# o and dq with V and K as the moving operand in a one-core attention backward kernel

## The chip, the cores and the metric

The kernel runs on one core of a Trainium2 chip. A core has TensorE (PE in the profile, PEld for its weight loads), VectorE (DVE), ScalarE (ACT), GpSimd (POOL) and SyncE (SP); the last two mostly order transfers here. The metric is the device time of one execution in microseconds, lower is better.

## What is computed

A decode step and its gradients: one token, attention over a cache of 4096 keys in 32 heads of 128, a dense layer with the mish activation beside it, and a gate that mixes both. The forward part:

```python
def _A_ref(x, k_cache, v_cache, wq, wo):
    B, Sq, D = x.shape
    H, Dh = 32, 128
    q = (lambda x, *d: x.transpose(*d))((x @ wq).reshape(B, Sq, H, Dh), 0, 2, 1, 3)
    scores = jnp.einsum("bhqd,bhkd->bhqk", q, k_cache) * (Dh ** -0.5)
    p = _softmax(scores, axis=-1)
    o = jnp.einsum("bhqk,bhkd->bhqd", p, v_cache)
    return (lambda x, *d: x.transpose(*d))(o, 0, 2, 1, 3).reshape(B, Sq, H * Dh) @ wo
...
x = A_x
g = _sigmoid((x * gate_w).sum(-1, keepdims=True))
a = _A_ref(x, A_k_cache, A_v_cache, A_wq, A_wo)
b = _B_ref(x, B_w1, B_b1, B_w2)
return g * a + (1 - g) * b
```

The outputs are this value and, by `jax.vjp` with a given `grad_out`, the gradients of x, both caches and all weights. Per head that means, with do the gradient of o: dP = V do, ds = p (dP - sum of dP p), dK = ds q, dV = p do, and dq = K^T ds. D is 640, everything is in bfloat16. K, V, dK and dV are 1 MB per head each and make up most of the traffic.

## The kernel before

One period of the loop (`period(h)`) treats one head. Its K and V lie in SBUF as 128 partitions x 32 columns of keys (J = 32) x 128 (Dh): key p*32 + j is at partition p, column j. Each of kts and vts has four buffers; the loads of head h+3 are ordered on SP's queue before period h, and a load waits until the last reader of its buffer is done. For K that reader is the dq product, for V the o product.

The order on each engine is written out by hand (`manual_schedule`); every engine works through its own list in order. The steps of one period:

- Scores of the next head. K is transposed on TensorE in four chunks of four FP32 transposes, each of which carries a pair of bfloat16 columns (`transposes`, lines 575 to 583). ACT copies a chunk out of PSUM as tT (line 582), and eight products (`products`, line 589) with 48 moving columns write the scores to the PSUM tile sA. `k_chunk` and `s_chunk` do this for head h+1 during period h. The same is done with V of head h, as `V(c)` and `dP(c)`, into the tile sB.
- Softmax of head h: the maximum m (line 664), its transpose over partitions (668), negM (670), e = exp(S - M) (675), the sum Z by a product with ones (678), zs (680), 1/Z as rz (682), p (684).
- o (`o_part`, line 660): 32 products accumulate in one PSUM region. Column j of V (128 x 128) is the stationary operand, column j of e is the moving one, broadcast to W = 48 equal columns, of which one is used. In the same way dq (line 713) takes K and ds.
- pj (691) sums dP times e, PT (694) transposes the partial sums, dj (700) adds them, ds (702) follows.
- dV and dK are outer products on VectorE, in two halves each (line 605); dK of head h is made in period h+1. Their stores go out on POOL's queue.
- `slot(h)` takes a few steps out of a list of other work (the dense layer, q, the gradients of wq and wo) on TensorE and VectorE.

sA has two buffers and sB one; each is one PSUM bank of 512 FP32 columns, in which scores, Z, o and the transpose of m, or dP, dq and PT, have their own columns.

Of the kernel before, what the change touches and what calls it, by code (L numbers as in the profile page):

```python
# [8 lines left out]
ALU = mybir.AluOpType  # L9
AX = mybir.AxisListType  # L10
F32 = mybir.dt.float32
# [5 lines left out]
def kernel(  # L17
# [24 lines left out]
    nc = tc.nc  # L42
    P = 128
    _, H, Sk, Dh = A_k_cache.shape
    D = A_x.shape[-1]
    F = B_w1.shape[1]
    J = Sk // P
    RC = D // P
    G = 4
    W = 48  # L50
# [40 lines left out]
    small = ctx.enter_context(tc.tile_pool(name="small", bufs=3))  # L91
# [21 lines left out]
    kts, vts, wqs, wos = {}, {}, {}, {}  # L113
# [26 lines left out]
    def load_w2(c):  # L140
# [25 lines left out]
    ident_f = const.tile([P, P], F32, name="ident_f")  # L166
    nc.gpsimd.memset(ident_f[:], 0.0)
    nc.gpsimd.affine_select(
        out=ident_f[:], in_=ident_f[:], compare_op=ALU.not_equal, fill=1.0,
# [69 lines left out]
    for i in range(3):  # L239
        t = const.tile([P, 2, G, 2, 2], BF16, name=f"qd2_{i}")  # L240
# [13 lines left out]
    def slot(h, p=2, d=1):  # L254

        slot_no[0] += 1
        room = {"P": p, "D": d, "T": 99}
        for kind in ("T", "D", "P"):
            for st in list(steps):
                name, k, fn, deps, head = st  # L260
                if k != kind or head > h or not room[k]:
                    continue
                if all(done.get(x, 1 << 30) < slot_no[0] for x in deps):
                    fn()
                    done[name] = slot_no[0]
                    steps.remove(st)
                    room[k] -= 1
# [63 lines left out]
    o_all = const.tile([P, H], BF16, name="o_all")  # L331
    dq_all = const.tile([P, H], BF16, name="dq_all")
# [242 lines left out]
    def transposes(src, c):  # L575
        tp = tr_ps.tile([P, 4, P], F32, name="tr", tag="tr")
        flat = f32v(src[:].rearrange("p j d -> p (j d)"))
        for t in range(4):
            k = c * 4 + t
            nc.tensor.transpose(tp[:, t, :], flat[:, k * P:(k + 1) * P], ident_f[:])  # L580
        sb = tsb.tile([P, 4, P], F32, name="tT", tag="tT")
        nc.scalar.copy(sb[:].rearrange("p a b -> p (a b)"), tp[:].rearrange("p a b -> p (a b)"))  # L582
        return sb[:].rearrange("p a b -> p (a b)").bitcast(BF16).rearrange("p (a b two) -> p a two b", a=4, two=2)

    def products(out, tb, c, vec):
        for t in range(4):
            k = c * 4 + t
            for par in range(2):
                nc.tensor.matmul(out[:, 2 * k:2 * k + W], lhsT=tb[:, t, par, :],  # L589
                                 rhs=vec[:, par, :].unsqueeze(1).to_broadcast([P, W // 2, 2]),  # L590
                                 start=(par == 0), stop=(par == 1))

    def k_chunk(h, c, ts):
        ts.append(transposes(kts[h], c))

    def s_chunk(h, c, ts):
        gp = gps[h // G]
        if c == 0:
            sts[h] = {"A": sa_ps.tile([P, 512], F32, name="sA", tag="sA")}
        products(sts[h]["A"][:, 0:J + W], ts[c], c, gp["x2"][:, 0, h % G])  # L600
# [10 lines left out]
    def dk_half(h, half):  # L611
        if h < 0:
            return
        st = sts[h]
        if half == 0:
            st["dK"] = outs.tile([P, J, Dh], BF16, name="dK_sb", tag="dVK")
        outer(st["dK"], st["ds"], gps[h // G]["qd"][:, 0, (h % G) * Dh:(h % G + 1) * Dh], half)
        if h == H - 1:
            a, b = half * (J // 2), (half + 1) * (J // 2)
            ring(h).dma_start(dKv[h][:, a:b, :], st["dK"][:, a:b, :])  # L620
        elif half == 1:
            ring(h).dma_start(dKv[h], st["dK"][:])  # L622
        if half == 1:
            sts.pop(h)

    def dv_half(h, half):
        st = sts[h]
        if half == 0:
            st["dV"] = outs.tile([P, J, Dh], BF16, name="dV_sb", tag="dVK")
        outer(st["dV"], st["p"], gps[h // G]["qd"][:, 1, (h % G) * Dh:(h % G + 1) * Dh], half)  # L630
        if half == 1:
            if h % 7 == 5 and h < H - 3:
                spread(h // 7, dVv[h], st["dV"])
            else:
                ring(h).dma_start(dVv[h], st["dV"][:])  # L635
# [9 lines left out]
    def period(h):  # L645
        gp = gps[h // G]
        st = sts[h]
        nxt = h + 1 < H
        A = st["A"]
        S, Z, O, MM = A[:, 0:J], A[:, 96:96 + J], A[:, 128:128 + W], A[:, 256:384]  # L650
        B = st["B"] = sb_ps.tile([P, 512], F32, name="sB", tag="sB")
        DP, DQ, PT = B[:, 0:J + W], B[:, 128:128 + W], B[:, 256:384]
        vec = gp["x2"][:, 1, h % G]
        tv, tk = [], []
        V = lambda c: tv.append(transposes(vts[h], c))
        dP = lambda c: products(DP, tv[c], c, vec)

        def o_part(a, b):
            for j in range(a, b):
                nc.tensor.matmul(O, lhsT=vts[h][:, j, :], rhs=st["e"][:, j:j + 1].to_broadcast([P, W]),  # L660
                                 start=(j == 0), stop=(j == J - 1))

        m32 = small.tile([P, 1], F32, name="m32", tag="m32")
        nc.vector.reduce_max(m32[:], S, axis=AX.X)  # L664
        V(0)
        dk_half(h - 1, 0)
        V(1)
        nc.tensor.transpose(MM, m32[:].to_broadcast([P, P]), ident_f[:])
        negM = small.tile([P, 1], F32, name="negM", tag="negM")
        nc.vector.tensor_reduce(negM[:], MM, axis=AX.X, op=ALU.max, negate=True)  # L670
        dk_half(h - 1, 1)
        e = st["e"] = small.tile([P, J], BF16, name="e_bf", tag="e_bf")
        V(2)
        dP(0)
        nc.scalar.activation(e[:], S, ACT.Exp, bias=negM[:], scale=1.0)
        V(3)
        dP(1)
        nc.tensor.matmul(Z, lhsT=ones_bf[:], rhs=e[:], start=True, stop=True)
        zs = small.tile([P, 1], F32, name="zs", tag="zs")
        nc.vector.reduce_sum(zs[:], Z, axis=AX.X)  # L680
        rz = st["rz"] = small.tile([P, 1], F32, name="rz", tag="rz")
        nc.vector.reciprocal(rz[:], zs[:])  # L682
        p_bf = st["p"] = small.tile([P, J, 2], BF16, name="p_bf", tag="p_bf")
        nc.scalar.activation(p_bf[:], e[:].unsqueeze(2).to_broadcast([P, J, 2]), ACT.Copy, scale=rz[:])  # L684
        dP(2)
        o_part(0, J)
        dP(3)
        slot(h)
        part = small.tile([P, 1], F32, name="part", tag="part")
        pj = small.tile([P, J], F32, name="pj", tag="pj", bufs=1)  # L690
        nc.vector.scalar_tensor_tensor(pj[:], in0=DP[:, 0:J], scalar=1.0, in1=e[:], op0=ALU.mult, op1=ALU.mult,
                                       accum_out=part[:])
        dv_half(h, 0)
        nc.tensor.transpose(PT, part[:].to_broadcast([P, P]), ident_f[:])  # L694
        if nxt:
            k_chunk(h + 1, 0, tk)
            k_chunk(h + 1, 1, tk)
        dd = small.tile([P, 1], F32, name="dd", tag="dd")
        dj = small.tile([P, P], F32, name="dj", tag="dj", bufs=1)
        nc.vector.tensor_scalar(dj[:], PT, rz[:], None, ALU.mult, ALU.add, accum_out=dd[:])  # L700
        ds = st["ds"] = small.tile([P, J, 2], BF16, name="ds_bf", tag="ds_bf")
        nc.vector.scalar_tensor_tensor(ds[:], in0=DP[:, 0:J].unsqueeze(2).to_broadcast([P, J, 2]), scalar=dd[:], in1=p_bf[:],  # L702
                                       op0=ALU.subtract, op1=ALU.mult)
        dv_half(h, 1)
        nc.vector.tensor_scalar(o_all[:, h:h + 1], O[:, 0:1], rz[:], None, ALU.mult)  # L705
        if nxt:
            s_chunk(h + 1, 0, tk)
            k_chunk(h + 1, 2, tk)
        slot(h)
        if nxt:  # L710
            s_chunk(h + 1, 1, tk)
        for j in range(J):
            nc.tensor.matmul(DQ, lhsT=kts[h][:, j, :], rhs=ds[:, j, 0:1].to_broadcast([P, W]),  # L713
                             start=(j == 0), stop=(j == J - 1))
        if nxt:
            k_chunk(h + 1, 3, tk)
            s_chunk(h + 1, 2, tk)
        nc.scalar.copy(dq_all[:, h:h + 1], DQ[:, 0:1])  # L718
        if nxt:
            s_chunk(h + 1, 3, tk)  # L720
        kts.pop(h)
        vts.pop(h)
        slot(h, 2, 2)
# [131 lines left out]
```

## Time and profile before

| | |
|---|---|
| median of 3 runs | 402.33 us (402.27 to 402.36) |
| the profiled execution | 402.56 us |
| its span, first to last instruction | 400.8 us |
| granted TensorE clock, mean | 0.913 |
| data moved by DMA | 164.92 MB, mean 412 GB/s |
| o products (line 660) | 1024, record of one 183 ns |
| dq products (line 713) | 1024, record of one 183 ns, a few at 215 |
| one head, from m to m | 9.2 to 12.1 us, four heads 15.8 to 21.3 us |

The records of products overlap, as they are pipelined: how fast they run is read from the distance of their starts, not from the length of a record. In the timeline a line has the start and the length in us, the engine, the source line, the operation, what it writes and reads, and in brackets how long the engine stood idle before it and whose end released it. In the waits a line says which instruction waited for which, then the total in us, how often, and the longest. A table of stretches has each engine's busy time in each stretch, the granted clock, the share of the DMA engines and the rate.

### The profile page before, as it was taken

What the parts mean: (1) busy time and instruction counts of PE and PEld (TensorE: products, weight loads), DVE (VectorE), ACT (ScalarE), POOL (GpSimd) and SP (SyncE); (2) the same over time, 40 slices, a digit from 0 to 9 for tenths busy, and PEclk for the clock granted to TensorE, in tenths of its full rate; (3) what the DMA queues carried; (4) which work ended last, traced back from release to release, by engine and by line L of the source; (5) the groups of instructions that cost most, each with busy time, mean ns of one, the idle gap of its engine ahead of it and who ended that gap; (6) DMA issues with size and microseconds to landing.
All of it is one profiled execution on the core that took longest, in us unless ns stands there. A gap on an engine that the chain in (4) does not pass through costs nothing.

```text
span 400.8 us, 13361 instructions
## 1 busy us (share of the span) xinstructions
PE 301.0 (75%) x5752; PEld 266.0 (66%) x5752; DVE 303.1 (76%) x783; ACT 178.2 (44%) x403; POOL 47.0 (12%) x94
## 2 busy tenths in 40 slices
PE   0788888678888788768879788838888888888300
PEld 0577888567777677658868778718777678877200
DVE  3339666556799999767658999836999997898860
ACT  1455454325545555326533555604545545555000
POOL 0001111021110111211110112101111121111000
PEclk9899999959999999969977999967999999999755
DMA  8999999999999999999999999999999999999995
GB/s 292 417 407 405 418 426 421 407 423 421 424 421 424 422 422 416 422 424 424 419 424 426 422 422 417 417 425 424 421 421 424 424 423 418 425 420 418 424 383 229
DMA packets 28359, 164.92 MB, mean 412 GB/s; under 512 B 3260, under 2 KB 3964, under 8 KB 12556
## 3 DMA queue, kind: packets, MB, share of 16 engines
q1 hardware_dynamic: 17136, 93.41, 56.5%
q0 software_dynamic: 11104, 70.64, 42.3%
q8 instruction: 45, 0.74, 0.7%
q14 instruction: 14, 0.11, 0.1%
q10 hardware_dynamic: 60, 0.01, 0.0%
HBM read 82.03 MB, written 82.03 MB: 409 GB/s over the span
## 4 chain that ended last, share of the span: by engine, by line
DVE 38%; DMA 32%; PE 20%; ACT 5%; issue 3%; ACTq 0%; SPq 0%
DMA Kn<-in_A_k_cache_dram 30%; DVE dK_sb L605 9%; DVE dV_sb L605 9%; PE tr L580 8%; DVE junk L378 5%; ACT tT L582 4%; DVE junk L278 3%; PE sA L660 3%; PE sA L589 3%; PE sB L713 3%; DVE junk L530 2%; DVE wo_g L367 1%; DMA vec_rows<-in_gate_w_dram 1%; DVE dj L700 1%; DVE dwq_t L732 1%
## 5 line engine op out<-in xcount | busy, mean ns | idle before, releaser
L582 ACT COPY tT<-tr 128x512 f32<-128x512 f32 x256 | 142.4, 587 | 127.8 <-PE tr L580 126.0
L589 PEld LDWEIGHTS <-tT 128*128 128x128 bf16 x2048 | 79.8, 98 | 40.3 <-ACT tT L582 34.6
L580 PE MATMUL tr<-ident_f,Kn 128*128 128x128 f32 x512 | 81.6, 297 | 9.2 <-DMA Kn<-in_A_k_cache_dram 9.2
L605 DVE TENSOR_TENSOR dV_sb<-p_bf,qd 128x2048 bf16<-128x2048 bf16 x64 | 78.0, 1218 | 0.2 <-issue 0.2
L605 DVE TENSOR_TENSOR dK_sb<-ds_bf,qd 128x2048 bf16<-128x2048 bf16 x64 | 77.7, 1216 | 0.0
L580 PE MATMUL tr<-ident_f,Vn 128*128 128x128 f32 x512 | 72.9, 278 | 0.0
L580 PEld LDWEIGHTS tr<-ident_f,Kn 128*128 128x128 f32 x512 | 61.0, 152 | 10.4 <-issue 10.4
L589 PE MATMUL sA<-qd,tT 128*128 128x48 bf16 x1024 | 48.7, 187 | 23.8 <-ACT dq_all L718 12.7
L580 PEld LDWEIGHTS tr<-ident_f,Vn 128*128 128x128 f32 x512 | 56.3, 142 | 0.0
L589 PE MATMUL sB<-qd,tT 128*128 128x48 bf16 x1024 | 46.0, 183 | 0.0
L660 PEld LDWEIGHTS <-Vn 128*128 128x128 bf16 x1024 | 30.2, 95 | 10.9 <-issue 10.9
L660 PE MATMUL sA<-e_bf,Vn 128*128 128x48 bf16 x1024 | 30.7, 183 | 8.1 <-DVE zs L680 6.5
L622 POOL DMA_DIRECT2D out_dram<-dK_sb x30 | 17.2, 574 | 138.9 <-DVE rz L682 86.5
L713 PE MATMUL sB<-ds_bf,Kn 128*128 128x48 bf16 x1024 | 32.2, 186 | 1.4 <-DVE ds_bf L702 1.4
L664 DVE TENSOR_REDUCE m<-sA 128x1 f32<-128x32 f32 x32 | 6.1, 189 | 32.9 <-PE sA L589 26.4
L713 PEld LDWEIGHTS <-Kn 128*128 128x128 bf16 x1024 | 29.5, 98 | 1.6 <-issue 1.6
L635 POOL DMA_DIRECT2D out_dram<-dV_sb x26 | 14.1, 542 | 135.8 <-DVE o_all L705 53.4
L278 DVE SCALAR_TENSOR_TENSOR junk<-wo_g,da_bc 128x640 bf16<-128x640 bf16 x32 | 26.2, 820 | 1.7 <-ACT da_bc L229 1.1
L378 DVE SCALAR_TENSOR_TENSOR junk<-wq_g,dq_bc 128x1024 bf16<-128x1024 bf16 (+1 forms) x25 | 25.1, 1005 | 0.2
L700 DVE TENSOR_SCALAR_CACHE_REDUCE dj<-sB,rz 128x128 f32<-128x128 f32 x32 | 11.1, 346 | 13.2 <-PE sB L694 13.2
L289 PE MATMUL q_ps<-wq_g,cols_bf 128*128 128x512 bf16 x40 | 13.1, 469 | 10.5 <-DMA wq_g<-in_A_wq_dram 10.5
L684 ACT ACTIVATE p_bf<-e_bf,rz 128x64 bf16<-128x64 bf16 x32 | 11.1, 348 | 13.9 <-DVE rz L682 11.1
(148 smaller groups left out, 268.8 us busy)
## 6 DMA issues: line engine op xcount, KB each, us to landing
Kn<-in_A_k_cache_dram SPq DMA_DIRECT2D x32, 1024.0 KB, 24.0
Vn<-in_A_v_cache_dram SPq DMA_DIRECT2D x32, 1024.0 KB, 28.0
out_dram<-dK_sb POOLq DMA_DIRECT2D x30, 1024.0 KB, 11.8
out_dram<-dV_sb POOLq DMA_DIRECT2D x26, 1024.0 KB, 11.8
wq_g<-in_A_wq_dram SPq DMA_DIRECT2D x4, 1280.0 KB, 23.2
wo_g<-in_A_wo_dram SPq DMA_DIRECT2D x8, 640.0 KB, 17.6
out_dram<-wo_g POOLq DMA_DIRECT2D x7, 640.0 KB, 11.8
out_dram<-dwq_t SPq DMA_DIRECT2D x4, 896.0 KB, 17.5
```

The costliest lines, as they stand in the source:

```text
L278: nc.vector.scalar_tensor_tensor(junk[:, 0:D], in0=wos[g][:, i, :], scalar=1.0, in1=da_bc[:], op0=ALU.mult, op1=ALU.mult, accum_out=gp["do ...
L289: nc.tensor.matmul(q_ps[:], lhsT=x_bf[:, rc:rc + 1].to_broadcast([P, P]), rhs=wq[:, rc, off:off + GD], start=(rc == 0), stop=(rc == RC - 1))
L378: nc.vector.scalar_tensor_tensor(junk[:, c0:c1], in0=wqs[w][:, rc, c0:c1], scalar=1.0, in1=dq_bc[:, w * WG * Dh + c0:w * WG * Dh + c1], op ...
L580: nc.tensor.transpose(tp[:, t, :], flat[:, k * P:(k + 1) * P], ident_f[:])
L582: nc.scalar.copy(sb[:].rearrange("p a b -> p (a b)"), tp[:].rearrange("p a b -> p (a b)"))
L589: nc.tensor.matmul(out[:, 2 * k:2 * k + W], lhsT=tb[:, t, par, :], rhs=vec[:, par, :].unsqueeze(1).to_broadcast([P, W // 2, 2]), start=(pa ...
L605: nc.vector.tensor_tensor(dst[:, a:b, :].rearrange("p j (a b) -> p j a b", b=2), col[:, a:b, :].unsqueeze(2).to_broadcast([P, n, Dh // 2, 2]),
L622: ring(h).dma_start(dKv[h], st["dK"][:])
L635: ring(h).dma_start(dVv[h], st["dV"][:])
L660: nc.tensor.matmul(O, lhsT=vts[h][:, j, :], rhs=st["e"][:, j:j + 1].to_broadcast([P, W]), start=(j == 0), stop=(j == J - 1))
L700: nc.vector.tensor_scalar(dj[:], PT, rz[:], None, ALU.mult, ALU.add, accum_out=dd[:])
L713: nc.tensor.matmul(DQ, lhsT=kts[h][:, j, :], rhs=ds[:, j, 0:1].to_broadcast([P, W]), start=(j == 0), stop=(j == J - 1))
```

## The change

o and dq are now made by `rows2`: two columns of e (or ds) are the stationary operand, two columns of V (or K), 256 elements side by side, are the moving one. Sixteen products accumulate a tile of 2 x 256 in PSUM. Row i, half i of it (the diagonal of 2 x 2 blocks) are the wanted sums over even and odd j; the other two blocks are not used. ACT copies the tile to SBUF as FP32, and `column` turns the two wanted rows into one column of 128 partitions with two FP32 products, whose moving operand is one column of a 2 x 2 identity. The places in the PSUM banks are dealt out anew. For o the column comes after the first `slot(h)`, before the part transpose; for dq it comes between `s_chunk(h + 1, 2)` and `s_chunk(h + 1, 3)`.

```diff
-        S, Z, O, MM = A[:, 0:J], A[:, 96:96 + J], A[:, 128:128 + W], A[:, 256:384]
+        S, Z, O, MM = A[:, 0:J], A[:, 96:96 + J], A[:, 88:89], A[:, 128:256]
+        O2 = A[0:2, 256:512]
         B = st["B"] = sb_ps.tile([P, 512], F32, name="sB", tag="sB")
-        DP, DQ, PT = B[:, 0:J + W], B[:, 128:128 + W], B[:, 256:384]
+        DP, DQ, PT = B[:, 0:J + W], B[:, 88:89], B[:, 128:256]
+        DQ2 = B[0:2, 256:512]
...
-        def o_part(a, b):
-            for j in range(a, b):
-                nc.tensor.matmul(O, lhsT=vts[h][:, j, :], rhs=st["e"][:, j:j + 1].to_broadcast([P, W]),
-                                 start=(j == 0), stop=(j == J - 1))
+        def rows2(out, cols, src):
+            for j in range(0, J, 2):
+                nc.tensor.matmul(out, lhsT=cols[:, j:j + 2], rhs=src[:, j:j + 2, :].rearrange("p j d -> p (j d)"),
+                                 start=(j == 0), stop=(j == J - 2))
+            t = small.tile([2, 2, Dh], F32, name="r2", tag="r2", bufs=2)
+            nc.scalar.copy(t[:].rearrange("i j d -> i (j d)"), out)
+            return t
+
+        def column(out, t):
+            for i in range(2):
+                nc.tensor.matmul(out, lhsT=t[:, i, :], rhs=ident_f[0:2, i:i + 1], start=(i == 0), stop=(i == 1))
...
         dP(2)
-        o_part(0, J)
+        o2 = rows2(O2, e, vts[h])
         dP(3)
         slot(h)
+        column(O, o2)
...
-        nc.vector.tensor_scalar(o_all[:, h:h + 1], O[:, 0:1], rz[:], None, ALU.mult)
+        nc.vector.tensor_scalar(o_all[:, h:h + 1], O, rz[:], None, ALU.mult)
...
-        for j in range(J):
-            nc.tensor.matmul(DQ, lhsT=kts[h][:, j, :], rhs=ds[:, j, 0:1].to_broadcast([P, W]),
-                             start=(j == 0), stop=(j == J - 1))
+        dq2 = rows2(DQ2, ds[:, :, 0], kts[h])
         if nxt:
             k_chunk(h + 1, 3, tk)
             s_chunk(h + 1, 2, tk)
-        nc.scalar.copy(dq_all[:, h:h + 1], DQ[:, 0:1])
+        column(DQ, dq2)
+        nc.scalar.copy(dq_all[:, h:h + 1], DQ)
```

## The prediction, before the changed kernel had run

> **What bounds the kernel now.** I read the page first, then the waits, then nine stretches of the span beside each other, then one undisturbed head in the timeline.
>
> ```profile
> PE 301.0 (75%) x5752; PEld 266.0 (66%) x5752; DVE 303.1 (76%) x783; ACT 178.2 (44%) x403; POOL 47.0 (12%) x94
> PEclk9899999959999999969977999967999999999755
> DMA  8999999999999999999999999999999999999995
> ```
>
> No engine is full, but the DMA row is: 164.92 MB at the 421 to 425 GB/s that most slices show are about 390 us, so transfers leave only some 10 us at the two ends. That looks like a kernel in which nothing else counts. The waits say otherwise:
>
> ```profile
> DVE m L664 <- PE sA L589: 26.4, 13, 5.2
> DVE pj L691 <- PE sB L589: 12.4, 18, 1.1
> PE q_ps L289 <- DMA wq_g<-in_A_wq_dram: 10.5, 3, 5.6
> PE tr L580 <- DMA Kn<-in_A_k_cache_dram: 9.2, 4, 3.3
> ```
>
> After its start the core waits for a load only seven times, 19.7 us in all (columns: total us, times, longest). The rest of the time TensorE (PE) and VectorE (DVE) drive each other, and the DMA is full because its queues hold loads ordered three heads ahead. The two bounds are nearly equal. The stretches show where the difference lies:
>
> ```profile
> core 0: us, PE busy (x) PEld busy (x) DVE busy (x) ACT busy (x) POOL busy (x), PEclk, DMA share, GB/s
> 71.55:90.30 18.75, 13.75 (x207) 11.42 (x206) 11.20 (x32) 5.58 (x12) 3.02 (x5) 0.73 1.02 417
> 162.85:180.00 17.15, 11.11 (x192) 9.63 (x191) 11.50 (x31) 5.58 (x12) 1.85 (x3) 0.80 1.02 423
> 198.60:214.40 15.80, 12.76 (x197) 11.34 (x196) 10.15 (x24) 5.37 (x12) 1.06 (x2) 0.69 1.01 421
> 256.50:277.80 21.30, 12.74 (x189) 10.34 (x187) 11.20 (x32) 5.64 (x12) 1.60 (x3) 0.68 1.02 425
> 277.80:367.30 89.50, 76.16 (x1555) 68.25 (x1553) 83.15 (x196) 47.74 (x108) 13.48 (x22) 1.00 1.01 421
> ```
>
> The first four are heads 5, 13, 16 and 21 (from one m of line 664 to the next). They take 15.8 to 21.3 us; their neighbours take 9.2 to 12.1. Their clock is 0.68 to 0.80, elsewhere it is 1.00: after the wait TensorE runs slowly for a while. What the loads cost is therefore the waits plus the slow work after them. Against similar heads: 18.75 - 10.6 = 8, 5.4 (its two waits, 2.05 + 3.33), 15.8 - 10.9 = 5, 21.3 - 10.9 = 10.5: together 29 us. That is all that a slower computation can hide in. The last row, nine heads (22 to 30), holds none of it: there the computation sets the pace.
>
> One head without a stall, number 15:
>
> ```profile
> 192.25 0.96 PE L660 MATMUL sA<-e_bf,Vn 128*128 128x48 bf16 x32
> 193.05 0.36 PE L589 MATMUL sB<-qd,tT 128*128 128x48 bf16 x8
> 193.45 0.19 DVE L691 SCALAR_TENSOR_TENSOR pj<-sB,e_bf 128x32 f32<-128x32 f32 x1 [1.05 <-PE sB L589]
> 193.70 0.32 PE L694 MATMUL sB<-ident_f,part 128*128 128x128 f32 x1 [0.29 <-DVE pj L691]
> ...
> 196.03 0.96 PE L713 MATMUL sB<-ds_bf,Kn 128*128 128x48 bf16 x32
> 196.83 0.64 PE L580 MATMUL tr<-ident_f,Kn 128*128 128x128 f32 x4
> ...
> 197.56 0.58 ACT L582 COPY tT<-tr 128x512 f32<-128x512 f32 x1 [0.95 <-PE tr L580]
> ...
> 198.20 0.37 PE L589 MATMUL sA<-qd,tT 128*128 128x48 bf16 x8 [0.54 <-ACT dq_all L718]
> ...
> 198.61 0.19 DVE L664 TENSOR_REDUCE m<-sA 128x1 f32<-128x32 f32 x1 [1.97 <-PE sA L589]
> ```
>
> TensorE is dense: o starts at 192.25 and the next group follows 0.80 us later, 32 products at 25 ns; dq the same (196.03 to 196.83). The last products of the next head's scores (198.20) release its m, for which VectorE has waited 1.97 us.
>
> **What the skill says.** "TensorE: Matmul & The Clock Gate", section "Back-to-back issue gap": N moving columns take N/2.4 + 2.5 ns, with a floor of about 25 ns at 64 columns or fewer. The trace agrees on both: 25 ns for these 48 columns, and for 512 columns
>
> ```profile
> 126.08 1.24 PE L289 MATMUL q_ps<-wq_g,cols_bf 128*128 128x512 bf16 x5
> ```
>
> less the 0.377 us record of the last, (1.24 - 0.377)/4 = 216 ns. Section "LDWEIGHTS (loading the stationary operand)": a load is priced by its columns, so two columns cost next to nothing; no load of two columns is in this trace, but those of 128 columns hide beside the products (0.80 us for 32 pairs). Section "Terms" says that transpose mode is four times faster for FP32; this trace has FP32 transposes alone, so an FP32 product that is none has to be bounded. Part 1 (the clock gate) has an idle array at half clock, which the stretches above show.
>
> **The change part by part**, warm clock.
>
> 1. Rows. 32 products at 25 ns go, 16 of 256 columns at 216/2 = 108 ns come: 1.73 against 0.80, +0.93 us on TensorE, for o and again for dq. The old form gained nothing from being narrow or wide: it sat on the 25 ns floor. The 32 large weight loads that go were hidden, so nothing is gained there.
>
> 2. Copy to SBUF by ScalarE (ACT), 2x256. Its row length is that of the 128x256 copy of line 373, mean 372 ns; I take 0.37. It waits for the last row product, whose record I put at 0.27 us, between 217 ns (128 columns, line 104) and 377 (512). ACT is busy 44% and has nothing urgent behind the o copy. Behind the dq copy stands the tT copy of K chunk 3.
>
> 3. Two small FP32 products per column. Cost c each. From below: 8 FP32 transposes start in 1.04 - 0.27 = 0.77 us, 0.11 each, load included. From above: four times that, 0.44, by the section "Terms". I take 0.25, since only the load is long and one column moves. A pair is 0.50.
>
> Head 15 with these. o's rows end at 193.98. dP(3) and pj shift by 0.93: pj starts at 194.38, and its result can go to PE at 194.63. The o copy runs from 193.87 + 0.27 + 0.04 = 194.18 to 194.55, so the column starts at 194.61: its wait hides beside the wait for pj, but its 0.50 does not. The part transpose (193.70) starts at 195.11, +1.41. DVE's second half starts 0.93 late and has dV to do while the transpose comes. dq would start at 197.44, its rows end at 199.17, and the four transposes run to 199.81. Its copy (199.37 to 199.74) clears ACT before tT needs it at 199.90; tT ends at 200.48 and the last products start at 200.54, against 198.20: **+2.34 us**. The dq column (199.80 to 200.35) lies inside the wait for tT and costs nothing as long as c is under 0.33. The copy of dq_all and o_all's new wait for ACT come long after their inputs. The K and V buffers come free about 1 to 2 us later, so loads are ordered later; with the DMA relieved they land sooner, so I charge nothing.
>
> Sum. Of heads 0 to 30, 17 have m starting at once after the last products: 17 x 2.34 = 39.8. In the other 14, VectorE has other work first (MLP rows, wq rows), and m comes 0.10 to 1.57 us after those products, 12.6 us in all: 14 x 2.34 - 12.6 = 20.2. Head 31 has no next scores: 1. Total +61. Less the stalls, 29: they are gone one after the other, since about 10 us have gathered by head 5. The computation ends 32 us later.
>
> Tail. Now the result rows are ordered at 388.2 and the span ends at 400.8, because stores of about 12 us stand in the queue. A computation that is slower than the DMA leaves less of a queue; with some 5 MB made in the last 14 us I take 6 of the 12.6 back (bounds 2 and 9). Span 400.8 + 61 - 29 - 6 = 426.8; the profiled run took 402.56, 1.8 over its span, so 428.6. That run is 0.2 above the median of 402.33: **428 us**.
>
> **Rivals.**
> - Cheap columns (c = 0.11): +2.05 per head, 17 x 2.05 + 14 x 2.05 - 12.1 = 51.4, total 420, with 9 of the tail 417; if the waits around a column also hide 0.2 us per head that I charge, 410. For it: one moving column. Against it: four passes.
> - Dear columns (c = 0.44): PT +1.79 and the dq column comes out of tT's shadow by 0.2, +2.9 per head, 77 in all, 445. Two-column loads that don't hide would end here or above.
> - The DMA floor, not slower: if a head grows by less than about 1.2 us, the 29 us before head 21 cover the first heads, and heads 22 to 30 use up the stores' 9 us at the end. Then 402 to 403, and a shorter tail could even bring 401. For it: the full DMA row. Against it: the rows alone are 1.86 us per head by a price that this trace shows.
>
> **How the numbers follow.** Forecast (421 to 440) 0.60, cheap 0.18 (409 to 421), dear 0.14, floor 0.08. A measurement here can tell 0.2% (0.8 us). Only the floor is not slower: same 0.04, faster 0.04. Range 409 to 446: it takes in both prices of the columns with the tail's bounds.
>
> **What would show it.** Right: row products 108 ns apart; heads like 15 near 11.6 us; no K or wq waits and no clock below 0.9 in mid-span; DMA slices under 9; VectorE's wait for m at 2 to 4 us per light head. Wrong: rows nearer 55 ns; column products off the estimate; stalls for K that stay although the heads got longer.

## The result and the profile after

| | before | after |
|---|---|---|
| median | 402.31 us (402.21 to 402.67, 6 runs) | 435.05 us (434.02 to 436.41, 6 runs) |
| ratio | | 1.0814, 95% interval 1.0793 to 1.0835 |
| profiled execution, its span | 402.56, 400.8 | 436.41, 434.6 |
| granted clock, mean | 0.913 | 0.976 |

The change costs 8%. The profiled execution of the kernel after is the slowest of its six, 1.4 us above their median. First the page of the kernel after: busy times, then the granted clock and the share of the DMA engines in 40 slices, and the row of the K loads in the table of transfers, which ends with the median time from order to landing (24.0 us before).

```profile
PE 394.8 (91%) x4977; PEld 327.0 (75%) x4984; DVE 305.2 (70%) x783; ACT 202.9 (47%) x467; POOL 47.0 (11%) x94
...
PEclk9999999999999999999998999999999999999975
DMA  8999999979999799999999799999999799996987
...
Kn<-in_A_k_cache_dram SPq DMA_DIRECT2D x32, 1024.0 KB, 9.9
```

TensorE is now the fullest engine (91%). The DMA row, which was an unbroken line of nines, has four sevens inside and a six near the end: there the transfers wait for the computation. A load lands 9.9 us after its order. That fewer transfers stand ahead of it fits this, but isn't shown by itself. The clock falls only once in mid-span (the 8), while in the kernel before it fell in the four heads with waits for loads, and these waits are gone. In the waits of the kernel after, no load holds up TensorE after the start; what has grown are VectorE's waits for TensorE (12.4 and 26.4 us before):

```profile
DVE pj L701 <- PE sB L589: 42.1, 32, 2.1
DVE m L673 <- PE sA L589: 40.4, 18, 5.6
```

Head 15 in the timeline of the kernel after (start, length, engine, line, operation):

```profile
214.19 1.91 PE L662 MATMUL sA<-Vn,e_bf 128*2 128x256 bf16 x16
...
216.03 0.37 PE L589 MATMUL sB<-qd,tT 128*128 128x48 bf16 x8
216.13 0.36 ACT L665 COPY r<-sA 2x256 f32<-2x256 f32 x1 [1.36 <-PE sA L662]
216.44 0.19 DVE L701 SCALAR_TENSOR_TENSOR pj<-sB,e_bf 128x32 f32<-128x32 f32 x1 [2.11 <-PE sB L589]
...
216.55 0.60 PE L670 MATMUL sA<-ident_f,r 2*128 2x1 f32 x4
...
217.08 0.32 PE L704 MATMUL sB<-ident_f,part 128*128 128x128 f32 x1
...
219.20 0.36 PE L589 MATMUL sA<-qd,tT 128*128 128x48 bf16 x8
...
219.49 1.91 PE L662 MATMUL sB<-Kn,ds_bf 128*2 128x256 bf16 x16
...
221.33 0.42 PEld L580 LDWEIGHTS tr<-ident_f,Kn 128*128 128x128 f32 x4 [0.22 <-issue]
221.33 0.66 PE L580 MATMUL tr<-ident_f,Kn 128*128 128x128 f32 x4
221.44 0.36 ACT L665 COPY r<-sB 2x256 f32<-2x256 f32 x1 [1.45 <-PE sB L662]
...
222.12 0.60 PE L670 MATMUL sB<-ident_f,r 2*128 2x1 f32 x4
...
222.72 0.37 PE L589 MATMUL sA<-qd,tT 128*128 128x48 bf16 x8
...
223.13 0.19 DVE L673 TENSOR_REDUCE m<-sA 128x1 f32<-128x32 f32 x1 [3.50 <-PE sA L589]
```

From the start of a set to the next work on TensorE it is now 1.84 us (214.19 to 216.03, 219.49 to 221.33), where it was 0.80. The column of o takes 0.53 (216.55 to 217.08). Of this, 0.14 us are hidden beside pj. In the kernel before, the part transpose starts 0.25 us after pj (193.45 to 193.70); here that would have been 216.69, and it starts at 217.08. So 0.39 us of the column count. From m to m this head takes 11.83 us for 9.25.

Added up (a stall is the wait for loads that made four heads long in the kernel before): the sum of the 27 heads without a stall grew by 59.4 us, the four with one shrank by 17.6, the first m came 0.55 later, the stretch from the last m to the order of the result rows grew by 1.1, and from there to the end it takes 3.0 us for 12.6. 59.4 - 17.6 + 0.55 + 1.1 - 9.6 = 33.85, the difference of the spans (434.6 - 400.8).

### The profile page after: what moved, and what is told of

It is laid out like the page before. It is cut to its first block, busy times and chain, and to the rows that moved or that the text cites. A ratio compares the mean times of both kernels' runs of the same rounds, so it can differ in the third digit from the quotient of the medians.

```text
span 434.6 us, 11913 instructions
## 1 busy us (share of the span) xinstructions
PE 394.8 (91%) x4977; PEld 327.0 (75%) x4984; DVE 305.2 (70%) x783; ACT 202.9 (47%) x467; POOL 47.0 (11%) x94
## 4 chain that ended last, share of the span: by engine, by line
PE 61%; DVE 27%; ACT 7%; issue 2%; DMA 1%; ACTq 0%; DVEq 0%
PE sA L662 14%; DVE dK_sb L605 12%; PE sB L662 12%; PE tr L580 11%; PE sA L589 7%; ACT tT L582 6%; PE sA L670 4%; PE sB L670 3%; DVE dV_sb L605 3%; DVE junk L378 2%; DVE junk L278 2%; PE sB L589 2%; PE q_ps L289 2%; PE sB L704 2%; DVE wo_g L367 1%
## 5 line engine op out<-in xcount | busy, mean ns | idle before, releaser
L582 ACT COPY tT<-tr 128x512 f32<-128x512 f32 x256 | 140.9, 587 | 79.6 <-PE tr L580 78.9
L589 PEld LDWEIGHTS <-tT 128*128 128x128 bf16 x2048 | 78.5, 97 | 31.0 <-ACT tT L582 15.8
L580 PE MATMUL tr<-ident_f,Kn 128*128 128x128 f32 x512 | 76.5, 283 | 0.0
L662 PE MATMUL sB<-Kn,ds_bf 128*2 128x256 bf16 x512 | 63.3, 279 | 1.0 <-DVE ds_bf L712 1.0
L662 PE MATMUL sA<-Vn,e_bf 128*2 128x256 bf16 x512 | 61.0, 272 | 3.5 <-DVE zs L689 1.2
L580 PEld LDWEIGHTS tr<-ident_f,Kn 128*128 128x128 f32 x512 | 57.3, 144 | 7.5 <-issue 7.5
L662 PEld LDWEIGHTS <-e_bf 128*2 128x2 bf16 x512 | 42.6, 83 | 15.9 <-issue 1.2
L662 PEld LDWEIGHTS <-ds_bf 128*2 128x2 bf16 x512 | 41.1, 85 | 14.7 <-DVE ds_bf L712 1.2
L665 ACT COPY r<-sB 2x256 f32<-2x256 f32 x32 | 11.6, 361 | 55.8 <-PE sB L662 52.9
L701 DVE SCALAR_TENSOR_TENSOR pj<-sB,e_bf 128x32 f32<-128x32 f32 x32 | 6.1, 191 | 42.1 <-PE sB L589 42.1
L665 ACT COPY r<-sA 2x256 f32<-2x256 f32 x32 | 11.6, 361 | 43.4 <-PE sA L662 43.4
```

Of the source, the lines that this page charges most:

```text
L662: nc.tensor.matmul(out, lhsT=cols[:, j:j + 2], rhs=src[:, j:j + 2, :].rearrange("p j d -> p (j d)"), start=(j == 0), stop=(j == J - 2))
L665: nc.scalar.copy(t[:].rearrange("i j d -> i (j d)"), out)
```

## The experiments

Three theories stood against each other. Theory 1 is the prediction's: TensorE's own line got longer, and the full queues of transfers cover a part; the time that these set, however fast the computation, is called the floor. Theory 2: the wide products read 256 columns a time out of SBUF and slow the transfers. Theory 3: the products are harmless, and the round trip from TensorE to ScalarE and back costs. All ratios are to the kernel before, run in between on the same chip; the growth of a light head is that of head 15 (9.25 us before).

| kernel | median us | ratio (95% interval) | light head |
|---|---|---|---|
| the change | 435.05 | 1.0814 (1.0793 to 1.0835) | +2.59 |
| wide o alone | 408.14 | 1.0139 (1.0124 to 1.0154) | +1.44 |
| wide dq alone | 402.65 | 1.0009 (1.0000 to 1.0019) | +1.15 |
| change, BF16 columns | 424.0 | 1.0533 (1.0517 to 1.0549) | +2.20 |
| change, half the rows | 400.48 | 0.9949 (0.9932 to 0.9965) | +0.84 |
| before, o twice | 406.67 | 1.0103 (1.0066 to 1.0139) | +0.81 |
| before, o and dq twice | 425.69 | 1.0576 (1.0519 to 1.0633) | +2.03 |
| before, o and dq three times | 504.03 | 1.2472 (1.2395 to 1.2549) | +3.22 |
| before, 128 columns | 417.13 | 1.0367 (1.0348 to 1.0385) | +2.03 |
| before, 192 columns | 470.56 | 1.1691 (1.1646 to 1.1735) | +3.74 |
| four column groups | 400.02 | 0.9938 (0.9923 to 0.9952) | -0.37 |

**One half of the change at a time.** Wide o alone:

```diff
-        dq2 = rows2(DQ2, ds[:, :, 0], kts[h])
+        DQN = B[:, 256:256 + W]
+        for j in range(J):
+            nc.tensor.matmul(DQN, lhsT=kts[h][:, j, :], rhs=ds[:, j, 0:1].to_broadcast([P, W]),
+                             start=(j == 0), stop=(j == J - 1))
...
-        column(DQ, dq2)
-        nc.scalar.copy(dq_all[:, h:h + 1], DQ)
+        nc.scalar.copy(dq_all[:, h:h + 1], DQN[:, 0:1])
```

> o in the new form (rows, copy, column), dq in the old narrow one. Theory 1 (TensorE's line: rows and column count, less what the transfers' floor hides): a head without a stall grows by 1.04 (rows 1.84 for 0.80) + 0.53 (column) = 1.6 us; over 31 heads about 39, less 27 of stalls and 8 of the tail: 406 to 410 us. Theory 2 (the wide products slow the transfers by reading SBUF): half of the change's reads, half of its growth, 418. Theory 3 (the round trip TensorE, ScalarE, TensorE is what costs): half the trips, 418.

Wide dq alone is the mirror of it (`o_all` then reads column 0 of ON):

```diff
-        o2 = rows2(O2, e, vts[h])
+        ON = A[:, 256:256 + W]
+        for j in range(J):
+            nc.tensor.matmul(ON, lhsT=vts[h][:, j, :], rhs=e[:, j:j + 1].to_broadcast([P, W]),
+                             start=(j == 0), stop=(j == J - 1))
...
-        column(O, o2)
```

> dq in the new form, o in the old one. Theory 1: +1.04 of rows, the column mostly beside the wait for tT, so 1.1 us per light head and nothing in heads where VectorE is behind; the stalls cover it: 402 to 405 us. Theories 2 and 3: 418, as for o.

Both times came out as theory 1 had them, 408.14 and 402.65; a light head grew by 1.44 with wide o, not by 1.6, as 0.14 of the column is hidden. In a light head the halves add up: 1.44 + 1.15 = 2.59. In the time they don't: +5.7 and +0.3 by themselves, +32.7 together. Theories 2 and 3, which wanted 418 twice, fall in this form. Whether either could still hold behind a floor is for the runs below. With wide dq alone the wait for loads has not gone everywhere. The waits of that kernel still have

```profile
PE q_ps L289 <- DMA wq_g<-in_A_wq_dram: 6.3, 1, 6.3
PE tr L580 <- DMA Kn<-in_A_k_cache_dram: 1.9, 1, 1.9
```

both in head 21. Heads 5, 13 and 16 are 15.8 us shorter than before, which pays for the growth of the heads around them: head 21 ends at 277.96 us, in the kernel before at 277.77. From there to the last m it takes 6.1 us more, and the tail behind it gives 5.0 back.

**The price of the columns.** The rows are copied as BF16 and picked with the BF16 identity:

```diff
-            t = small.tile([2, 2, Dh], F32, name="r2", tag="r2", bufs=2)
+            t = small.tile([2, 2, Dh], BF16, name="r2", tag="r2", bufs=2)
...
-                nc.tensor.matmul(out, lhsT=t[:, i, :], rhs=ident_f[0:2, i:i + 1], start=(i == 0), stop=(i == 1))
+                nc.tensor.matmul(out, lhsT=t[:, i, :], rhs=ident_bf[0:2, i:i + 1], start=(i == 0), stop=(i == 1))
```

> The changed kernel with the copied rows and the identity in BF16, so that a column is two BF16 products (o and dq are rounded once more on the way). Theory 1: the first column falls from 0.53 to about 0.1 and counts in every head, the second from 0.53 to 0.1 and was almost hidden: 0.45 to 0.5 us per head, 435 - 14 = 419 to 423 us. Theories 2 and 3: 434 to 436, since reads and trips stay.

424.0: 11 us less, a light head 0.39 us shorter. Expected were 0.45 to 0.5 and 419 to 423, so the size was missed: the 0.14 us beside pj had been hidden already, and the rest, 0.39, is gone. Copies and waits stayed, so theory 3 has no room for these 11 us.

**The price of the rows.**

```diff
-            for j in range(0, J, 2):
+            for j in range(0, J // 2, 2):
...
-                                 start=(j == 0), stop=(j == J - 2))
+                                 start=(j == 0), stop=(j == J // 2 - 2))
```

> The changed kernel with only the first 8 of the 16 row products in o and in dq; the second half of the keys is left out of o and dq. Theory 1: each set falls by 8 x 0.109 = 0.87, the head's growth from 2.58 to 0.84, which the floor of the transfers covers: 402 to 405 us, not 435 - 54. Theory 2: half the reads, 418. Theory 3: all trips stay, 430 or more.

400.48, with +0.84 in the light head as worked out. All copies, columns and waits are still there: 16 products less per head (8 of each set) are worth 35 us, of which the last part can't be seen, because the transfers end no sooner. It lies under its expectation (402 to 405) and is even 0.5% below the kernel before, which no theory had; it comes back below.

**Doses on the kernel before.** If theory 1 is right, any TensorE work put into the kernel before must show the same floor. The first three issue the narrow products again. Shown is the kernel with both twice; o twice has only the added `o_part`, and both three times has two of them and `range(3)`:

```diff
         o_part(0, J)
+        o_part(0, J)
...
-        for j in range(J):
+        for j in [j for _ in range(2) for j in range(J)]:
```

> The kernel before with the 32 narrow o products issued twice (the second pass starts the sum anew, so values are the same). A dose of 0.80 us of TensorE per head. Theory 1 (29 us of stalls and some 9 of the tail cover a growth): 0.8 us in light heads, about 19 us in all, covered: 401 to 404 us. Rival (TensorE's time adds to the end, 32 x 0.8): 425 or more.

> The kernel before with o and dq products issued twice, 1.60 us per head. Theory 1: about 39 us, less 27 and 8: 404 to 410 us. Rival (all adds): 450.

> The kernel before with o and dq products issued three times, 3.20 us per head. Theory 1: past the floor each us per head counts in nearly every head: about 86 us, less 27 and 9.6: 448 to 458 us. Theory 2 (it is the wide reads of SBUF that slow the change): narrow products at this dose should cost less than the change does, below 435.

Three misses: 406.67, 425.69 and 504.03 (498 to 509). Many light heads grew by just the dose (0.80 where o is issued twice), but others by far more: at three times, heads 14 and 19 grew by 7.15 and 7.58 us instead of 3.2. The waits of that kernel (o and dq three times) show a kind that the kernel before doesn't have, of products (PE) and of weight loads (PEld) inside a set:

```profile
PEld L715 <- issue: 12.6, 12, 2.5
PE sA L660 <- issue: 9.9, 8, 2.3
PE sB L715 <- issue: 9.7, 9, 2.3
```

"issue" means that the engine stood still and nothing in the profile released it. In the middle of a set there are gaps of up to 2.5 us: 18 of them, 11 us together, where both are issued twice, and 20 with 23 us where it is three times. These kernels hold 15409, 17457 and 21553 instructions for 13361 before, and the instruction queue brought 53, 61 and 77 packets for 45. So a dose with no instruction more was needed: the same products, but with the column of e or ds broadcast wider, to 128 columns as shown or to 192 (the results then lie at other columns of their PSUM tiles).

```diff
-                nc.tensor.matmul(O, lhsT=vts[h][:, j, :], rhs=st["e"][:, j:j + 1].to_broadcast([P, W]),
+                nc.tensor.matmul(O, lhsT=vts[h][:, j, :], rhs=st["e"][:, j:j + 1].to_broadcast([P, 128]),
...
-            nc.tensor.matmul(DQ, lhsT=kts[h][:, j, :], rhs=ds[:, j, 0:1].to_broadcast([P, W]),
+            nc.tensor.matmul(DQ, lhsT=kts[h][:, j, :], rhs=ds[:, j, 0:1].to_broadcast([P, 128]),
```

> The kernel before with the moving column of e or ds broadcast to 128 columns in place of 48, so a narrow product should take about 54 ns instead of 25 and a set 1.73 us instead of 0.80, with not one instruction more and without the copy and column of the change. Theory 1 (TensorE's line against the transfers' floor): 1.86 us per light head, about 19 us later at the last m, tail 9 shorter: 409 to 416 us. If the issued-twice kernel (425.7 at 1.6 us per head) was slow because of its time on TensorE, this one is above it, 428 or more; if it was slow because of its many instructions, this one is well below it.

> The same with 192 columns: about 81 ns, a set 2.6 us, 3.6 to 3.7 us more per light head. Theory 1, scaled from the change (2.58 per light head, 435): 1.1 us more in 31 heads, 462 to 472 us. If TensorE's time alone explains the issued-thrice kernel (504 at 3.2 us), this one is above 504.

417.13, a little over its expectation (a product takes 58 ns for the 54 reckoned), and 470.56, inside it. At 128 columns a set takes 1.83 us, as the change's does (timeline of that kernel):

```profile
205.15 2.00 PE L660 MATMUL sA<-e_bf,Vn 128*128 128x128 bf16 x32
206.98 0.36 PE L589 MATMUL sB<-qd,tT 128*128 128x48 bf16 x8
```

Light heads grow by 2.03 and 3.74, evenly, and there is no gap inside a set. The doses without instructions thus lie below those with them, though their time on TensorE is larger: 417 for 426, 471 for 504. So the loss of the repeated kernels beyond their dose isn't TensorE's time for the columns; it goes with the number of products and weight loads issued, which no run keeps apart. That the fetching of instructions is what runs dry is argued from the gaps and the packets, and wasn't measured by itself. The wide dose also answers theory 2 from the other side: it reads no wide rows of V or K as the moving operand, keeps the old weight loads, has neither copy nor column, and loses 15 us by its time on TensorE alone.

**Four column groups.** The row products go to four groups of 32 output partitions. Two columns of e are padded to 32 by simply taking the 30 that follow (the tile is 30 columns longer, zeros at its end); only two rows of each group are used. The column is made by two BF16 products over all 128 partitions, which pick these rows and add the groups.

```diff
-                nc.tensor.matmul(out, lhsT=cols[:, j:j + 2], rhs=src[:, j:j + 2, :].rearrange("p j d -> p (j d)"),
-                                 start=(j == 0), stop=(j == J - 2))
-            t = small.tile([2, 2, Dh], F32, name="r2", tag="r2", bufs=2)
+                a = (j // 2 % 4) * 32
+                nc.tensor.matmul(out[a:a + 32, :], lhsT=cols[:, j:j + 32],
+                                 rhs=src[:, j:j + 2, :].rearrange("p j d -> p (j d)"),
+                                 start=(j < 8), stop=(j >= J - 8))
+            t = small.tile([P, 2, Dh], BF16, name="r2", tag="r2", bufs=2)
...
-                nc.tensor.matmul(out, lhsT=t[:, i, :], rhs=ident_f[0:2, i:i + 1], start=(i == 0), stop=(i == 1))
+                nc.tensor.matmul(out, lhsT=t[:, i, :], rhs=pick[:, i:i + 1], start=(i == 0), stop=(i == 1))
```

> The changed kernel with the row products dealt out to the four groups of 32 output partitions (32 columns of e or ds as the stationary operand, of which two count), so that four products run beside each other, and the column made by two BF16 products over 128 partitions, which also add the four groups. Theory 1: rows 4 x 0.109 + 0.2 = 0.6 to 0.7 us for 1.84, columns 0.1 to 0.15: TensorE has a little less per head than before the change, and the transfers set the end: 399 to 403 us. If the groups don't run beside each other, rows stay at 1.84 and it is near the kernel with BF16 columns, 424.

400.02, inside the expectation. Its timeline in head 15:

```profile
191.04 0.62 PE L673 MATMUL sA<-Vn,e_pad 128*32 128x256 bf16 x16
...
191.60 0.37 PE L599 MATMUL sB<-qd,tT 128*128 128x48 bf16 x8
...
192.14 0.20 PE L682 MATMUL sA<-pick,r 128*128 128x1 bf16 x2 [0.17 <-ACT r L677]
...
192.26 0.32 PE L716 MATMUL sB<-ident_f,part 128*128 128x128 f32 x1
```

A set takes 0.56 us (191.04 to 191.60), a third of the change's and less than the old 0.80; the column takes 0.12. This kernel reads the same wide rows of V and K as the change, in less time, copies a larger tile (128 x 256) and makes the same trips: neither theory 2 nor theory 3 leaves room for that. With BF16 columns alone it was 424.0, so 24 us of the way to 400 are the groups'. The gain is small. Heads in which VectorE sets the pace gain nothing (head 9 takes 11.84 us as before), so the 27 heads give 4.7 us in all, and the four with waits for loads, which are back, take 1.5 of them. The waits of this kernel (19.7 us before):

```profile
PE q_ps L299 <- DMA wq_g<-in_A_wq_dram: 13.6, 3, 6.7
PE tr L590 <- DMA Kn<-in_A_k_cache_dram: 7.5, 4, 2.4
```

It is 0.6% below the kernel before: its last m comes 3.1 us earlier and the tail after it is 0.7 longer. The kernel with half the rows has its last m 1.7 us later and a tail that is 3.6 shorter. So near the floor 2 us can come from either end; why the transfers could be done 2 us sooner in these two isn't settled.

## Why the prediction was right

The measured time lies in the main case (421 to 440); 428 was forecast, 435.05 came. By its steps:

- **What bounds the kernel.** Right: beyond a hidden dose TensorE's line sets the time, as the runs with more and with less work on it show. The stalls that a slower computation could hide in were put at 29 us. In the change the four heads shrank by 17.6 where -19.6 was forecast (4 x 2.34 less 29), 2.0 off. Most of this is head 16, whose dq set fell into a stretch at half clock (below).
- **Rows**, +0.93 per set: the products run 109 ns apart, as forecast, but a set takes 1.84 and not 1.73 us. After the last product, the first weight load of 128 columns starts late: the weight load shows 0.22 us of "issue" there (the line at 221.33), and the next product comes 0.20 after the last row product. The dq set also begins late: 0.11 us after the last product ahead of it, where that distance was 0.025. The four other kernels whose dq set has stationary operands of 2 or 32 columns show the same at both ends, and wide o alone, whose dq set has 128, does not. The prediction had no term for it. The price of the rows came from the Trainium skill, "TensorE: Matmul & The Clock Gate", section "Back-to-back issue gap", which gives it for isolated products, and for streams of load and product about 81 ns at 128 columns and 131 at 512; the streams of these runs follow the formula instead, with 58 ns at 128 and 216 at 512. The 32 weight loads that went gave nothing, as said.
- **Copy**, 0.37: 0.36 measured, and hidden in both places.
- **Columns**, 0.50: 0.53 measured. The upper bound came from the Trainium skill, "TensorE: Matmul & The Clock Gate", section "Terms", which calls the transpose mode four times faster for FP32. The trace has four pairs of load and product for the two products, 0.11 us each: twice the cost of a transpose (0.11), not four times, in this form; no run has the same product in transpose mode to compare. Of o's column 0.39 us count, where 0.48 were reckoned.
- **A light head**: +2.59 for +2.34. The part transpose comes 0.03 later than reckoned: the late load behind o's set lies beside the copy and the column's wait, so it costs nothing more. The dq set begins 0.09 late and its end adds 0.11; the last 0.02 is the copy to tT.
- **Sum.** The 27 heads without a stall: 59.4 for 50.6 (13 x 2.34 + 20.2). This is the term that was mis-sized. The 13 heads whose m followed at once grew by 33.0 for 30.4. The 14 with other work on VectorE grew by 26.4 for 20.2: from m to the last products TensorE's line grew by 37.7 us there, not by 32.8 (14 x 2.34), most by the 0.25 per head just named, and in heads 7, 8, 9, 25 and 29 by 2.8 to 3.3 us. And 1.1 of the 12.6 us of cover was not taken up: in heads 9, 17 and 25 m still came about 0.36 us after the last products could release it. So head 9 was to grow by 0.8 and grew by 2.11, head 25 by 0.8 and grew by 1.67. Why TensorE's line grew by more in these five is open.
- **Tail**: 6 us back were forecast with bounds 2 and 9; 9.6 came back, outside them. Only 3.0 us lie between the order of the result rows and the end.
- **The floor's turning point.** Put at 1.2 us per head. Wide dq alone (+1.15) costs 0.1%, wide o alone (+1.44) costs 1.4%. Right.
- **The signs named beforehand.** Row products 109 ns apart (108 forecast), head 15 at 11.83 us (11.6), no wait for K or wq, DMA slices under 9, m's wait in head 15 at 3.50 us (2 to 4). One failed: the clock did fall under 0.9 in mid-span, to 0.89 over head 16.

These misses of size, 8.8 and 2.0 us up, 3.6 down and 0.6 at the start, make up the 7.8 us between the forecast span of 426.8 and the measured 434.6. That it wasn't more is in part luck: the tail's miss took 3.6 us off the others.

## What to carry to other kernels

A full DMA row doesn't mean that compute is free: add up the stalls for loads, the slow work after them and what the queue at the end can give back, and that is about the dose that is hidden; beyond it a head's growth counts nearly in full, so half of a change can cost nothing and the whole of it 8%. Count TensorE products by their distance: 48 moving columns cost 25 ns and 256 cost 109, so turning the operands round traded 32 products for 16 at four times the price, while the weight loads that went had been hidden. Products with few useful output rows paid off here only when four of them ran in separate column groups.

## What the runs showed of the hardware

- Four column groups run beside each other in full: four products start 3 to 4 ns apart and the next four 0.11 us later, so 16 products of 256 columns take 0.56 us up to the next work, 1.84 in one group.
- A dq set whose stationary operands have 2 or 32 columns starts and ends about 0.09 us late (0.11 and 0.20 us to the neighbouring product, for 0.025 and 0.11) where the work on both sides loads 128.
- Many short products in a row can cost more than their array time. With 64 or 96 narrow products in a row, 25 ns apart, TensorE stood still inside the sets, up to 2.5 us at a time, waiting for nothing that the profile shows. 32 products with 192 moving columns, which take longer in all than 96 of the narrow ones, had no gap.
- In head 16 of the change the granted clock fell to half for 3.41 us in the midst of work, with no wait for a load before it. The dq set there takes 3.33 us as a record where 1.91 is usual. Before it stand 25 products of one moving column each. It came at the same place with 192 columns (3.41 us) and with half the rows (6.83 us). Seven other kernels have the same 25 products and no such stretch in head 16, so these products alone don't bring it about; the cause is open.
